# Product P1 of the gate is copied into the gate's PSUM bank, and nine matmuls accumulate on the copy

## The chip, the cores and the metric

The kernel runs on one core of a Trainium2 chip. The metric is the time of one execution on the device in microseconds (us), the median of three runs. Inside the core there are five engines with a program each, all in order: TensorE (PE, matrix products; its weight loads are listed apart as PEld), VectorE (DVE), ScalarE (ACT), GpSimd (POOL) and SyncE (SP). The last two mostly start transfers (DMA) here.

## The reference

The input x has 2048 tokens of 640 values. It is normalised (mean and variance per token), and three things are added: x itself, the real part of a two-dimensional Fourier transform of the normalised x, and a gated feed-forward layer of it.

```python
xn = layernorm(x)                                    # 2048 x 640
a, b = xn @ hid_re.T, xn @ hid_im.T                  # Fourier transform along the hidden axis
A = seq_re @ a - seq_im @ b                          # and along the tokens, real part
gate, up = xn @ W_gate, xn @ W_up                    # 640 x 1728 each
B = (relu(gate) * up) @ W_down                       # 1728 x 640
out = x + A + B
```

All is float32. The kernel keeps that precision by splitting each operand into a high and a low part and making three matmuls of one: high by high, high by low, low by high (`mm3`, lines 136 to 141).

## The kernel before

The program has three stages that follow each other on PE: the token transform (to 405 us of the profile), gate and up (405 to 730 us), and the last stage that multiplies by W_down and the hidden Fourier matrix and writes the output. The change is in the second.

**Gate and up** works through 26 units: 13 tiles of 128 columns of W_gate and W_up, for each half of the tokens. A unit computes a 128 x 1024 tile of relu(gate) * up. It does not make the block products one by one, but by a scheme of the Strassen-Winograd kind: sums and differences of the weight blocks (`Weights.sums`, five DVE operations on tile `z`, L861 to L865) and of the token blocks (made earlier, the tiles `xs_early`, `r` and `sets_b`) are multiplied, and the products are added in several ways. P1 = A11·B11 is such a product; it is needed in more than one result.

**One unit on PE** (`gate_up`, lines 917 to 968). A unit uses three PSUM banks, `b1`, `b2` and `b4`, 128 x 512 each. Its matmuls, in order: 6 into `b1` (P1); 9 into the `b1` of the unit before (`last_products(n - 1)`, not in unit 0); 9 into `b2` (A12·B21 and A4·X4); 9 into `b4` (S1·T1 and U4·X4); 6 on top of `b1` (S2·T2); 3 on top of `b4` (G4·X4); 6 on top of `b4` (S4·B22); 6 on top of `b1` (S3·T3). That is 54. Some of them cannot start before another engine has read the bank: the 6 of S2·T2 must wait for the copy of `b1`, and the 3 of G4·X4 for the copy of `b4` into `ob` (L954, shown as `ob<-ps` on ACT).

**One unit on ACT.** In this order: `copy(p1, b1)` (`p<-ps`, PSUM to SBUF), the high part of the next unit's weights in two pieces (`ahead.high(0)`, `gw<-z` of 1024 columns, and `ahead.high(1)`, `gw<-z` of 1152), `copy(ob, b4)`, `copy(u2, b1)` (`u<-ps`) and `copy(u3, b1)` (`u<-ps`). Between u3 and the next unit's p1 stand the ACT steps of side work: `besides[n]` and `urgent[n]`, which prepare tokens and weights for later (lines 1113 to 1132).

**One unit on DVE.** `ahead.sums()`; then `finals(n - 1)`, three operations that finish the unit before (L886 and twice L888: relu of the gate times up, for both column halves); then L945, which adds `b2` and p1 into the first half of `oa`; the low parts of the next unit's weights (`gw<-z,gw`, L875, twice; the second needs `ahead.high(1)`); L963, which adds `b4` and u2 into the second half of `oa`; then the side work of `besides[n]`.

**What sets the order.** PE, DVE and ACT are pinned to the order in which the program is written (`tc.manual_schedule(engines=PINNED)`, L1162). The Tile layer only adds the waits. The tiles p1, u2, u3 and oa come from pool `tmp` that has one buffer for each name (L839), so `oa` of unit n lies where `oa` of unit n - 1 lies, which `finals(n - 1)` still reads.

Of the kernel before, what the change touches and what calls it, by code (L numbers as in the profile page):

```python
# [10 lines left out]
OP = mybir.AluOpType  # L11
# [5 lines left out]
W2 = 2 * CH  # L17
# [19 lines left out]
B11, B12, B21, B22, T1, T2, T3, T4, X4 = range(9)  # L37
# [5 lines left out]
A11, A12, A22 = (2 * P * i for i in range(3))  # L43
A4, U4, G4 = (6 * P + P * i for i in range(3))
# [21 lines left out]
def fnet_reglu_kernel(  # L66
# [56 lines left out]
    def bank():  # L123
        return psum_p.tile([P, CH], F32, name="ps")
# [4 lines left out]
    def copy(o, i):  # L129
        return nc.scalar.activation(o, i, AF.Copy)  # L130
# [715 lines left out]
    tt = nc.vector.tensor_tensor  # L846
# [33 lines left out]
    tmp = lambda name, n=CH: pool("tmp").tile([P, n], F32, name=name)  # L880
    c0, c1 = slice(0, CH), slice(CH, W2)

    def finals(n):

        u3, oa, ob, b1 = held.pop(n)
        tt(ob[:, c1], ob[:, c1], u3, op=OP.add)  # L886
        for c, up in ((c1, ob[:, c1]), (c0, b1)):
            nc.vector.scalar_tensor_tensor(ob[:, c], oa[:, c], 0.0, up, op0=OP.max, op1=OP.mult)  # L888
        with tc.issue_after(nc.gpsimd.dma_start(hd[1 - n // NF][n % NF], ob).ins):
            for f in behind_store[n]:  # L890
                f()
# [3 lines left out]
    def products(n):  # L895

        q, w = 1 - n // NF, weights[n].w

        def block(ps, a, b, first, last, more=False):
            for j in range(2):  # L900
                o = a + j * P
                mm3(ps, (w[:, 0, o : o + P], w[:, 1, o : o + P]), set_half(q, b, j),
                    first and j == 0, last and j == 1, more)

        def block4(ps, a, c, last, more=False):
            mm3(ps, (w[:, 0, a : a + P], w[:, 1, a : a + P]), set_half(q, X4, c), False, last, more)

        return block, block4

    def last_products(n):  # L910

        block, block4 = products(n)
        b1 = held[n][-1]
        block(b1, A22, T4, False, False, True)
        block4(b1, U4, 0, True, True)

    def gate_up(n):
        ahead = weights.get(n + 1)

        def the_rest():  # L920
            if ahead:
                ahead.high(1)
                ahead.low(0)
                ahead.low(1)

        block, block4 = products(n)
        for f in issues[n]:
            f()
        b1, b2, b4 = bank(), bank(), bank()
        block(b1, A11, B11, True, True)  # L930
        if ahead:
            ahead.sums()
        if n > 0:
            last_products(n - 1)
            finals(n - 1)
        p1, u2, u3, oa = tmp("p1"), tmp("u2"), tmp("u3"), tmp("oa", W2)
        ob = pool("hob").tile([P, W2], F32, name="ob")
        for f in urgent[n]:
            f()
        copy(p1, b1)  # L940
        if ahead:
            ahead.high(0)
        block(b2, A12, B21, True, False)
        block4(b2, A4, 0, True)
        tt(oa[:, c0], b2, p1, op=OP.add)  # L945
        if n > 0:
            the_rest()
        if n + 2 < NU:
            weights[n + 2] = Weights(n + 2)
        for f in loads[n]:  # L950
            f()
        block(b4, S1, T1, True, False)
        block4(b4, U4, 1, True)
        copy(ob[:, c1], b4)  # L954
        if n == 0:
            the_rest()
        block(b1, S2, T2, False, True, True)
        copy(u2, b1)
        for f in midway[n]:
            f()  # L960
        block4(b4, G4, 1, False, True)
        block(b4, S4, B22, False, True, True)
        held["dve"] = tt(oa[:, c1], b4, u2, op=OP.add)  # L963
        block(b1, S3, T3, False, True, True)
        held["act"] = copy(u3, b1)
        for f in besides[n]:
            f()
        held[n] = u3, oa, ob, b1
# [193 lines left out]
    with tc.manual_schedule(engines=PINNED):  # L1162
        third[0]()
        fourth_set[0]()
        weights[0] = Weights(0)
        rest_weights()
        weights[1] = Weights(1)
        weights[0].high(0)
        weights[0].low(0)
        weights[0].sums()  # L1170
        third[1]()
        weights[0].high(1)
        weights[0].low(1)
        gate_up_rest(1, None)
        for n in range(NU):
            gate_up(n)
        for f in issues[NU]:
            f()
        gate_up_rest(0, NU - 1)
# [394 lines left out]
```

## Time and profile before

| what | value |
|---|---|
| time, median of 3 runs (lowest, highest) | 1022.85 us (1022.72, 1023.73) |
| span of the profiled execution, first to last instruction | 1021.1 us |
| outside the span, against the median | 1.75 us |
| PE busy | 1015.6 us, 4510 matmuls |
| DVE busy | 823.5 us |
| ACT busy | 454.9 us |
| gate and up | 405.2 to 730 us |

A row of the timeline is: start (us), duration (us), engine, line, operation, names of what is written and read, shapes, count, and in brackets the idle time of the engine just before, with the instruction that ended it. A row of the waits is: who waited for whom, total us, number of times, longest us. A row of a window is: the stretch, its length, busy time and instruction count of each engine, granted clock, DMA share, GB/s. Where matmuls follow each other without a gap, their starts are 0.227 us apart, though each is recorded with a duration of 0.39 us, since they overlap in the pipeline.

### The profile page before, as it was taken

The page shows a single profiled execution, that of the slowest core. Times are in us where ns is not written, and L with a number is a line of the kernel's source. Part 1 is how long each engine was busy: PE and PEld are TensorE (multiplying, and loading weights), DVE is VectorE, ACT ScalarE, POOL GpSimd, SP SyncE. Part 2 cuts the span into 40 slices and gives each one's busy share as a digit, 9 for nine tenths or more (in the row PEclk, how much of TensorE's full clock was granted, in tenths as well). Part 3 has the DMA queues.
Part 4 walks back from the last instruction along what each step waited for, and adds up shares of the span by engine and source line. Part 5 has one row for each costly group of instructions (what it writes and reads, how often), then busy time and mean ns, then how long its engine had stood idle before and what let it go on. Part 6 is the DMA issues. An engine that isn't in the chain of part 4 may idle for free.

```text
span 1021.1 us, 12761 instructions
## 1 busy us (share of the span) xinstructions
PE 1015.6 (99%) x4510; PEld 840.8 (82%) x4510; DVE 823.5 (81%) x1162; ACT 454.9 (45%) x588; POOL 117.2 (11%) x189
## 2 busy tenths in 40 slices
PE   9999999999999999999999999999999999999998
PEld 7888888888888888888888888888888888888887
DVE  7967976969979697688888977787597888589887
ACT  6664453333334444434445444443443454454552
POOL 2000010121110001321111111111100000000001
PEclk9999999999999999999999999999999999999999
DMA  9884744976869666874658989899798879999784
GB/s 336 314 270 173 265 149 142 330 259 200 348 210 340 222 190 224 261 232 167 232 208 286 285 295 316 289 341 313 234 335 250 256 249 325 328 326 315 219 284 165
DMA packets 113872, 267.57 MB, mean 262 GB/s; under 512 B 13104, under 2 KB 58096, under 8 KB 112176
## 3 DMA queue, kind: packets, MB, share of 16 engines
q1 hardware_dynamic: 92416, 179.03, 52.5%
q0 software_dynamic: 20960, 87.31, 24.6%
q8 instruction: 35, 0.57, 0.2%
q10 hardware_dynamic: 432, 0.43, 0.1%
q14 instruction: 29, 0.24, 0.1%
HBM read 203.26 MB, written 72.89 MB: 270 GB/s over the span
## 4 chain that ended last, share of the span: by engine, by line
PE 99%; DMA 0%; ACT 0%; DVE 0%; SPq 0%; issue 0%
PE ps L140 32%; PE ps L139 32%; PE ps L141 32%; PE ps L527 3%; PE ps L556 1%; PE ps L1368 1%; DMA raw<-in_dft 0%; ACT cb L357 0%; ACT xs_early L258 0%; DVE y L1225 0%; SPq L596 0%; ACT mv L234 0%
## 5 line engine op out<-in xcount | busy, mean ns | idle before, releaser
L139 PE MATMUL ps<-cb,wt 128*128 128x512 f32 (+1 forms) x407 | 157.9, 388 | 0.0
L141 PE MATMUL ps<-cb,wt 128*128 128x512 f32 (+1 forms) x407 | 157.9, 388 | 0.0
L140 PE MATMUL ps<-cb,wt 128*128 128x512 f32 (+1 forms) x407 | 157.9, 388 | 0.0
L133 ACT ACTIVATE cb<-rw 128x1024 fp32r<-128x1024 f32 (+1 forms) x94 | 89.2, 960 | 77.1 <-PE ps L141 56.5
L134 DVE TENSOR_TENSOR cb<-rw,cb 128x1024 fp32r<-128x1024 f32 (+1 forms) x94 | 102.6, 1101 | 22.3 <-ACT cb L133 21.7
L133 ACT ACTIVATE cb<-raw 128x1024 fp32r<-128x1024 f32 x64 | 67.9, 1061 | 105.2 <-PE ps L141 97.0
L134 DVE TENSOR_TENSOR cb<-raw,cb 128x1024 fp32r<-128x1024 f32 x64 | 78.2, 1222 | 31.5 <-ACT cb L133 31.3
L141 PE MATMUL ps<-xs_early,gw 128*128 128x512 f32 x260 | 101.2, 389 | 0.0
L139 PE MATMUL ps<-xs_early,gw 128*128 128x512 f32 x260 | 101.2, 389 | 0.0
L140 PE MATMUL ps<-xs_early,gw 128*128 128x512 f32 x260 | 101.1, 389 | 0.0
L139 PE MATMUL ps<-cb,xs_late 128*128 128x512 f32 x232 | 90.2, 389 | 0.0
L140 PE MATMUL ps<-cb,xs_late 128*128 128x512 f32 x232 | 90.2, 389 | 0.0
L141 PE MATMUL ps<-cb,xs_late 128*128 128x512 f32 x232 | 90.2, 389 | 0.0
L139 PEld LDWEIGHTS ps<-cb,wt 128*128 128x128 f32 x407 | 76.4, 188 | 16.0 <-DVE y L1225 0.2
L141 PEld LDWEIGHTS ps<-cb,wt 128*128 128x128 f32 x407 | 76.4, 188 | 15.7
L140 PEld LDWEIGHTS ps<-cb,wt 128*128 128x128 f32 x407 | 76.4, 188 | 15.6
L139 PE MATMUL ps<-cb,xs_early 128*128 128x512 f32 x226 | 87.9, 389 | 0.0
L140 PE MATMUL ps<-cb,xs_early 128*128 128x512 f32 x226 | 87.9, 389 | 0.0
L141 PE MATMUL ps<-cb,xs_early 128*128 128x512 f32 x226 | 87.9, 389 | 0.0
L130 ACT ACTIVATE gw<-z 128x1024 fp32r<-128x1024 f32 (+1 forms) x52 | 56.4, 1110 | 38.6 <-PE ps L141 23.6
L130 ACT ACTIVATE u<-ps 128x512 f32<-128x512 f32 x52 | 31.1, 598 | 89.6 <-PE ps L141 77.7
L875 DVE TENSOR_TENSOR gw<-z,gw 128x1024 fp32r<-128x1024 f32 (+1 forms) x52 | 64.8, 1284 | 1.9 <-ACT gw L130 1.8
(209 smaller groups left out, 1989.4 us busy)
## 6 DMA issues: line engine op xcount, KB each, us to landing
raw<-in_dft SPq DMA_DIRECT2D x94, 512.0 KB, 5.4
wt<-wparts SPq DMA_DIRECT2D x74, 256.0 KB, 4.3
wparts<-pw POOLq DMA_DIRECT2D x12, 1408.0 KB, 7.9
z<-in_wgu SPq DMA_DIRECT2D x26, 640.0 KB, 5.6
rw<-hd SPq DMA_DIRECT2D x27, 512.0 KB, 6.2
hd<-ob POOLq DMA_DIRECT2D x26, 512.0 KB, 4.8
wt<-wparts SPq DMA_DIRECT2D x29, 384.0 KB, 5.4
rw<-pq SPq DMA_DIRECT2D x19, 512.0 KB, 6.4
```

The lines of the kernel that those rows point to most:

```text
L130: return nc.scalar.activation(o, i, AF.Copy)
L133: nc.scalar.activation(hi, src, AF.Copy)
L134: return nc.vector.tensor_tensor(lo, src, hi.bitcast(F32), op=OP.subtract)
L139: nc.tensor.matmul(ps, wh, mh, start=first, stop=False, skip_group_check=more)
L140: nc.tensor.matmul(ps, wh, ml, start=False, stop=False, skip_group_check=more)
L141: nc.tensor.matmul(ps, wl, mh, start=False, stop=last, skip_group_check=more)
L527: nc.tensor.matmul(E[0, key], xn_part(n * SG + j, d)[v == 1], b[:, int(v == 2), j], start=False, stop=n % NH == NH - 1 and (j, v) == (SG - ...
L556: nc.tensor.matmul(E[c, key], xn_part(j, d)[v == 1], b[c][0][:, int(v == 2), j], start=j == 0 and v == 0, stop=False)
L875: tt(self.w[:, 1, cs], self.z[:, cs], self.w[:, 0, cs].bitcast(F32), op=OP.subtract)
L1368: nc.tensor.matmul(B[out], w[:, v, oo : oo + P], b, start=False, stop=last and v == 1, skip_group_check=more)
```

## The change

Tile p1 is left out. ACT's copy of `b1` goes into bank `b2` (PSUM to PSUM), and the nine matmuls into `b2` no longer clear the bank at their first one, but accumulate on the copy. The sum is then in `b2`, so that DVE's L945 is left out, and ACT copies `b2` into the first half of `oa`.

```diff
-        p1, u2, u3, oa = tmp("p1"), tmp("u2"), tmp("u3"), tmp("oa", W2)
+        u2, u3, oa = tmp("u2"), tmp("u3"), tmp("oa", W2)
         ob = pool("hob").tile([P, W2], F32, name="ob")
         for f in urgent[n]:
             f()
-        copy(p1, b1)
+        copy(b2, b1)
         if ahead:
             ahead.high(0)
-        block(b2, A12, B21, True, False)
-        block4(b2, A4, 0, True)
-        tt(oa[:, c0], b2, p1, op=OP.add)
+        block(b2, A12, B21, False, False, True)
+        block4(b2, A4, 0, True, True)
+        copy(oa[:, c0], b2)
         if n > 0:
             the_rest()
```

`the_rest` is `ahead.high(1)`, `ahead.low(0)` and `ahead.low(1)`. In unit 0 it stands behind `copy(ob, b4)` instead.

How the order moves is seen in unit 1. On ACT, before (p, gw and ob as above, u_3292 is u2, u_3293 is u3):

```order
L130 ACTIVATE p_3291<-ps 128x512 [waits DVE_49,PE_49]
L130 ACTIVATE gw<-z 128x1024 [waits DMAHW1_49,PE_49]
L130 ACTIVATE gw<-z 128x1152 [waits DVE_49]
L130 ACTIVATE ob<-ps 128x512 [waits DMASW5_49,DMASW3_49,DMASW6_49,DMASW2_49,DMASW7_49,DMASW0_49,PE_49]
L130 ACTIVATE u_3292<-ps 128x512 [waits PE_49,Activation_49]
L130 ACTIVATE u_3293<-ps 128x512 [waits DVE_49,PE_49]
```

And with the change:

```order
L130 ACTIVATE ps<-ps 128x512 [waits PE_49]
L130 ACTIVATE gw<-z 128x1024 [waits DMAHW1_49,PE_49,Activation_49]
L130 ACTIVATE oa<-ps 128x512 [waits DVE_49,PE_49,Activation_49]
L130 ACTIVATE gw<-z 128x1152
L130 ACTIVATE ob<-ps 128x512 [waits PE_49]
L130 ACTIVATE u_3290<-ps 128x512 [waits PE_49,Activation_49]
L130 ACTIVATE u_3291<-ps 128x512 [waits PE_49,Activation_49]
```

A copy into `oa` has come between the two pieces of the high weights, ahead of the copy into `ob`, and it waits for DVE (the second L888 of the unit before is what reads the old `oa` last) and for PE.

On DVE, from the finals of unit 0 to L963 of unit 1, before:

```order
L886 TENSOR_TENSOR ob<-ob,u_3200 128x512 [waits Activation_49]
L888 SCALAR_TENSOR_TENSOR ob<-oa,ob 128x512 [waits DVE_49]
L888 SCALAR_TENSOR_TENSOR ob<-oa,ps 128x512 [waits PE_49]
L945 TENSOR_TENSOR oa<-ps,p_3291 128x512 [waits DVE_49,PE_49,Activation_49]
L875 TENSOR_TENSOR gw<-z,gw 128x1024 [waits Activation_49]
L875 TENSOR_TENSOR gw<-z,gw 128x1152 [waits Activation_49]
L963 TENSOR_TENSOR oa<-ps,u_3292 128x512 [waits PE_49,Activation_49]
```

And with the change:

```order
L886 TENSOR_TENSOR ob<-ob,u_3199 128x512 [waits Activation_49]
L888 SCALAR_TENSOR_TENSOR ob<-oa,ob 128x512 [waits DVE_49]
L888 SCALAR_TENSOR_TENSOR ob<-oa,ps 128x512 [waits PE_49]
L875 TENSOR_TENSOR gw<-z,gw 128x1024 [waits Activation_49]
L875 TENSOR_TENSOR gw<-z,gw 128x1152 [waits Activation_49]
L963 TENSOR_TENSOR oa<-ps,u_3290 128x512 [waits DVE_49,PE_49,Activation_49]
```

Only L945 is gone. PE keeps its order, and its first matmul into `b2` in unit 1 gets a wait on ACT. The last matmul of `last_products` and the first two of `b2`, with the change:

```order
L141 MATMUL ps<-xs_early,gw 128x512
L139 MATMUL ps<-xs_early,gw 128x512 [waits Activation_49]
L140 MATMUL ps<-xs_early,gw 128x512
L141 MATMUL ps<-xs_early,gw 128x512
L139 MATMUL ps<-xs_early,gw 128x512
```

Before, the same rows stand there without a wait.

## The prediction

> **What bounds the kernel now.** I read the page's totals and its chain first, then PE's own waits, then two windows of one unit each in gate and up (unit 10, which runs latest against PE, and unit 15, a quiet one).
>
> ```profile
> PE 1015.6 (99%) x4510; PEld 840.8 (82%) x4510; DVE 823.5 (81%) x1162; ACT 454.9 (45%) x588; POOL 117.2 (11%) x189
> PE 99%; DMA 0%; ACT 0%; DVE 0%; SPq 0%; issue 0%
> PE ps L121 <- DVE warm L117: 1.1, 1, 1.1
> PE ps L556 <- ACT xs_early L258: 0.7, 1, 0.7
> 525.56:537.85 12.29, 12.29 (x56) 10.06 (x54) 10.64 (x21) 5.86 (x8) 1.84 (x3) 1.00 0.67 237
> 586.81:599.05 12.24, 12.24 (x56) 10.14 (x54) 9.70 (x18) 5.27 (x7) 1.98 (x3) 1.00 0.87 284
> ```
>
> PE carries 99% of the chain, and in the whole execution it waits twice, 1.8 us in all, both times before 7 us. So in gate and up it never waits. Two things follow. Taking work from DVE cannot make PE faster, since PE waits for nobody there and its matmuls stay the same in number and order. And every moment in which the change makes PE wait is added to the end in full, because nothing later has slack in which to lose it. The question is only where PE now waits, and how long.
>
> **The clock of a unit.** A unit's 54 matmuls take 12.24 us, 0.2267 each. Unit 1 and unit 25 start at these rows:
>
> ```profile
> 415.40 0.39 PE L139 MATMUL ps<-xs_early,gw 128*128 128x512 f32 x1
> 709.21 0.39 PE L139 MATMUL ps<-xs_early,gw 128*128 128x512 f32 x1
> ```
>
> Their distance is 24 units of 12.24, plus the 0.05 by which unit 10 is longer. So unit n starts at T(n) = 415.40 + 12.24(n - 1), and 0.05 later from unit 11 on. By the counts in the program, `b2`'s nine matmuls start at T+3.40, the last of them at T+5.21, and G4's, which wait for the copy of `b4` into `ob`, at T+8.84. All times below are from T. Unit 10 (T = 525.56) shows how near ACT is to that edge already:
>
> ```profile
> 530.07 0.58 ACT L130 ACTIVATE p<-ps 128x512 f32<-128x512 f32 x1
> 530.54 1.05 ACT L130 ACTIVATE gw<-z 128x1024 fp32r<-128x1024 f32 x1
> 532.28 0.28 DVE L865 TENSOR_TENSOR z<-z 128x128 f32<-128x128 f32 x1
> 532.59 1.17 ACT L130 ACTIVATE gw<-z 128x1152 fp32r<-128x1152 f32 x1 [1.00 <-DVE z L865]
> 533.67 0.58 ACT L130 ACTIVATE ob<-ps 128x512 f32<-128x512 f32 x1
> 534.30 0.19 PEld L139 LDWEIGHTS ps<-xs_early,gw 128*128 128x128 f32 x1 [0.16 <-ACT ob L130]
> 534.40 0.39 PE L139 MATMUL ps<-xs_early,gw 128*128 128x512 f32 x1
> ```
>
> The copy into `ob` ends at 534.25; the weight load of G4 starts 0.05 later, its matmul 0.15 after the copy's end, at T+8.84, just on time. I take 0.16 from the end of an ACT copy to the matmul it releases. The rows also give ACT's pitch when it is back to back: an instruction starts 0.09 to 0.11 before the one ahead is recorded as ended (530.54 against 530.65; 533.67 against 533.76), and its delay behind a DVE end: 0.03 (L865 ends at 532.56, the second `gw<-z` starts at 532.59).
>
> **What is removed.** L945, 26 times:
>
> ```profile
> L945 DVE TENSOR_TENSOR oa<-ps,p 128x512 f32<-128x512 f32 x26 | 18.0, 692 | 7.3 <-PE ps L141 4.6
> L130 ACT ACTIVATE ob<-ps 128x512 f32<-128x512 f32 x26 | 15.5, 597 | 42.7 <-PE ps L141 42.7
> ```
>
> That is 18.0 us of DVE, and worth nothing by itself: PE hides it. Added are 26 ACT copies, PSUM to SBUF as the `ob` ones, so 0.6 each. ACT's total (45% of the span) has room. What counts is where the copy stands and what it waits for.
>
> **New wait 1: the copy into b2.** PE's first matmul of `b2` now needs the copy of `b1`. From unit 1 on, the nine matmuls of the unit before stand between (2.04 us). In unit 0 they do not:
>
> ```profile
> 406.76 0.60 ACT L130 ACTIVATE p<-ps 128x512 f32<-128x512 f32 x1 [0.76 <-PE ps L141]
> 406.56 0.39 PE L139 MATMUL ps<-xs_early,gw 128*128 128x512 f32 x1
> ```
>
> The copy ends at 407.36, PE can go on at 407.52 in place of 406.56: 0.96 us. A copy from PSUM to PSUM stands nowhere in the trace; it could take less than 0.6, hardly more than L945's 0.69, which moves this term by 0.1 at most. In later units the copy must end by T+3.24. In the latest, unit 10, it ends at 530.65, T+5.09: 1.85 late, because ACT does side work ahead of it.
>
> **New wait 2: the copy into oa.** It waits for the second L888 of the unit before, and behind it in ACT's queue are the second piece of high weights and then the copy into `ob`, for which PE's G4 waits. Before, nothing in front of `ob` on ACT waited for L888. If L888 ends at T+fe: the oa copy starts at fe + 0.03 (the delay behind a DVE end), the weights 0.50 later (0.59 less the 0.09 of overlap), the `ob` copy 1.08 after that (1.17 less 0.09), it takes 0.58, and PE goes on 0.16 later: fe + 2.35. PE should go on at 8.84. So PE stalls by fe - 6.49. The second L888 of each unit that comes near it (units 3 and 5 to 15):
>
> ```profile
> 446.38 0.68 DVE L888 SCALAR_TENSOR_TENSOR ob<-oa,ps 128x512 f32<-128x512 f32 x1
> 471.85 0.68 DVE L888 SCALAR_TENSOR_TENSOR ob<-oa,ps 128x512 f32<-128x512 f32 x1
> 483.06 0.68 DVE L888 SCALAR_TENSOR_TENSOR ob<-oa,ps 128x512 f32<-128x512 f32 x1
> 496.34 0.68 DVE L888 SCALAR_TENSOR_TENSOR ob<-oa,ps 128x512 f32<-128x512 f32 x1
> 509.14 0.68 DVE L888 SCALAR_TENSOR_TENSOR ob<-oa,ps 128x512 f32<-128x512 f32 x1
> 519.22 0.68 DVE L888 SCALAR_TENSOR_TENSOR ob<-oa,ps 128x512 f32<-128x512 f32 x1
> 533.81 0.68 DVE L888 SCALAR_TENSOR_TENSOR ob<-oa,ps 128x512 f32<-128x512 f32 x1
> 543.55 0.68 DVE L888 SCALAR_TENSOR_TENSOR ob<-oa,ps 128x512 f32<-128x512 f32 x1
> 557.19 0.68 DVE L888 SCALAR_TENSOR_TENSOR ob<-oa,ps 128x512 f32<-128x512 f32 x1
> 569.43 0.68 DVE L888 SCALAR_TENSOR_TENSOR ob<-oa,ps 128x512 f32<-128x512 f32 x1
> 580.76 0.68 DVE L888 SCALAR_TENSOR_TENSOR ob<-oa,ps 128x512 f32<-128x512 f32 x1
> 592.33 0.68 DVE L888 SCALAR_TENSOR_TENSOR ob<-oa,ps 128x512 f32<-128x512 f32 x1
> ```
>
> With their T, fe is 7.18, 8.17, 7.14, 8.18, 8.74, 6.58, 8.93, 6.38, 7.78, 7.78, 6.87 and 6.20. Some of this lateness is inherited: DVE comes late out of the unit before. A stall of PE there takes that part away, since DVE's L963 at the end of a unit then waits for PE again. L963 of units 5, 7, 8, 9 and 13:
>
> ```profile
> 475.68 0.68 DVE L963 TENSOR_TENSOR oa<-ps,u 128x512 f32<-128x512 f32 x1
> 500.16 0.68 DVE L963 TENSOR_TENSOR oa<-ps,u 128x512 f32<-128x512 f32 x1
> 512.96 0.68 DVE L963 TENSOR_TENSOR oa<-ps,u 128x512 f32<-128x512 f32 x1
> 524.47 0.69 DVE L963 TENSOR_TENSOR oa<-ps,u 128x512 f32<-128x512 f32 x1 [1.34 <-PE ps L141]
> 574.17 0.69 DVE L963 TENSOR_TENSOR oa<-ps,u 128x512 f32<-128x512 f32 x1
> ```
>
> Unit 9 is on time (T+11.15, DVE waits for PE); the others are at 11.32, 11.32, 11.88 and 11.84, late by 0.17, 0.17, 0.73 and 0.69. I take that off fe of units 6, 8, 9 and 14: 6.97, 8.57, 5.85, 6.18. The stalls by fe - 6.49 are then: unit 3 0.69, unit 5 1.68, unit 6 0.48, unit 7 1.69, unit 8 2.08, unit 10 2.44, units 12 and 13 1.29 each, the rest none; 11.64 in all. Units 16 to 24 do the same work as unit 15, with 0.29 to spare. Wait 1 is not added in these units: a stall at `b2` shifts G4's due time by as much, while the finals do not wait for `b2`, so the larger of the two counts (in unit 10, 2.44 over 1.85).
>
> After a hold-up PE needs a few matmuls to regain its pace; unit 10, where only a weight load was held, is 0.05 longer than unit 15 in the windows above. For nine stalls that is 0.45.
>
> **Sum.** 0.96 + 11.64 + 0.45 = 13.05 us. The profiled execution's span was 1021.1, so the new span is 1034.15; the median of the runs lies 1.75 above the span: 1035.9 us, 1.3% slower.
>
> What is late next: the second low part of the weights, on DVE behind the second high piece.
>
> ```profile
> L875 DVE TENSOR_TENSOR gw<-z,gw 128x1024 fp32r<-128x1024 f32 (+1 forms) x52 | 64.8, 1284 | 1.9 <-ACT gw L130 1.8
> ```
>
> It can start when that piece ends, at fe + 0.03 + 0.50 + 1.17 = fe + 1.70, and ends about 1.3 later, in unit 10 at 11.9; the next unit needs it at 12.24 plus the stall of 2.44: hidden, with over 2 us. The stores of `ob` follow the finals as before. No DMA is added or moved.
>
> **Rivals.**
>
> *Lateness cures itself.* If fe is late only because DVE trails from unit to unit, the first stalls let it catch up and later units find it on time: 0.96 + 0.69 = 1.7, so 1024.5 us, no difference. Units 6, 8, 9 and 14 speak for it. Against it: L963 of unit 9 waited 1.34 us for PE, so DVE was on time, and yet unit 10 has the latest fe; its lateness is made inside the unit, by side work. It decides if the same held for units 5, 7 and 12. 5%.
>
> *The freed 0.69 moves the finals.* If L945's time came off fe in each unit, the stalls would be 0, 0.99, 0, 1.00, 1.39, 1.75, 0.60, 0.60, 6.3 in all; with unit 0 and seven restarts 7.6, so 1030.5. Against it: between L945 and the next finals stands L963, which mostly waits for PE. 11%.
>
> *The chain from L888 to G4 is longer than by rows.* Each 0.1 on it costs eight stalls 0.1, and beyond 0.29 units 14 to 24 pay too: with 0.6 more, 8 x 0.6 + 11 x 0.3 = 8.1, so 1044; with 0.3 more, 1038.3. Nothing in the rows asks for it, but an ACT copy that waits for DVE and PE at once is not among them. 10%.
>
> *The clock drops.* The first matmuls of the execution run at half the pace of those that follow, and the column of the granted clock does not tell it:
>
> ```profile
> 1.05:4.45 3.40, 3.40 (x33) 3.40 (x34) 0.74 (x2) 1.49 (x2) 0.00 (x0) 1.00 0.75 213
> 4.45:5.29 0.84, 0.84 (x17) 0.82 (x15) 0.77 (x4) 0.63 (x3) 0.00 (x0) 1.00 0.98 246
> 6.20:10.20 4.00, 4.00 (x18) 3.27 (x19) 3.68 (x11) 2.38 (x6) 1.43 (x2) 1.00 1.04 407
> ```
>
> 33 matmuls of 128 columns in 3.40 us, then 17 in 0.84. If each of nine stalls led to 3.4 us at half pace, each would cost 1.7 more, 15 in all: 1051. Against it: after the 0.7 us wait at L556 the third window has 18 of 512 columns in 4.00 us, the full pace. [...] 3%.
>
> *Faster* would need PE to have waited before, and it did not: 1%.
>
> **How the numbers follow.** Forecast 1035.9 with 70%; its own uncertainty is 0.1 to 0.2 of a us on each of eight stalls and the inherited parts (had they not gone, 0.17 + 0.17 + 0.09 + 0.38 more), so 1034 to 1038. The range takes in the freed 0.69 below and the longer chain above: 1030 to 1041. A measurement of this kernel tells about 0.2% (2 us) from no change. Slower by more: 94%; within: 5%; faster: 1%.
>
> **What would show it.** In the new profile PE's waits list ACT: in unit 0 the `ps<-ps` copy, 0.7 to 1.0; in units 5, 7, 8, 10, 13 the same copy, and then in those and in 3, 6, 12 the `ob` copy. The `oa` copy's idle time is ended by DVE L888 in units 3 to 13 and by L888 too in 15 to 24, with no stall behind it. PE outside gate and up keeps its times. I would be wrong if quiet units stall, if matmuls after a stall start more than 0.24 apart, or if L888 moves against T.

## The result and the profile after

The changed kernel takes 1036.47 us (median of four runs, 1036.19 to 1036.78) against 1022.98 us before (four runs, 1022.72 to 1023.73): a ratio of 1.0129, 95% interval 1.0115 to 1.0144. The forecast was 1035.9 us in a range of 1030 to 1041. The profiled execution's span is 1034.4 us, 13.3 more than before.

The changed kernel's page (busy times, chain of waits), PE's waits (who waited for whom, total us, times, longest), and two groups of instructions (busy, mean ns, idle time just before and what ended it), with the row of L963 before the change behind them:

```profile
PE 1020.7 (99%) x4510; PEld 841.0 (81%) x4510; DVE 808.4 (78%) x1136; ACT 466.7 (45%) x614; POOL 117.3 (11%) x189
PE 90%; DVE 5%; ACT 2%; issue 2%; DMA 0%; POOL 0%; ACTq 0%; DVEq 0%; POOLq 0%
PE ps L139 <- ACT ps L130: 5.6, 6, 1.6
PE ps L139 <- ACT ob L130: 3.3, 7, 1.0
L130 ACT ACTIVATE oa<-ps 128x512 f32<-128x512 f32 x26 | 15.6, 599 | 51.4 <-DVE ob L888 43.6 <-PE ps L141 7.9
L963 DVE TENSOR_TENSOR oa<-ps,u 128x512 f32<-128x512 f32 x26 | 18.0, 691 | 48.2 <-PE ps L141 47.0 <-issue 1.2
```

```profile
L963 DVE TENSOR_TENSOR oa<-ps,u 128x512 f32<-128x512 f32 x26 | 17.9, 690 | 34.6 <-PE ps L141 34.6
```

DVE has become 15 us lighter and spends what it gained in waiting: its idle time before L963 went from 34.6 to 48.2 us. PE, which waited for nobody in gate and up, now waits for the two ACT copies that were named, 13 times. The chain of waits, 99% PE before, now passes through DVE and ACT for 7% of the span, with 2% of issue beside them. The two rows of waits sum to 8.9 us and not 13.3. Most of the difference is that they begin at the recorded end of the last matmul, 0.16 us after the next one was due, and that the matmul behind a wait is followed by the next only 0.34 us later in place of 0.23: for 13 waits that is 3.5 us of the 4.4.

Unit 10 in the timeline of the changed kernel (start, duration, engine, line, names; T = 533.51):

```profile
538.08 0.58 ACT L130 ACTIVATE ps<-ps 128x512 f32<-128x512 f32 x1
538.71 0.50 PE L139 MATMUL ps<-xs_early,gw 128*128 128x512 f32 x1 [1.64 <-ACT ps L130]
539.05 0.40 PE L140 MATMUL ps<-xs_early,gw 128*128 128x512 f32 x1
541.81 0.68 DVE L888 SCALAR_TENSOR_TENSOR ob<-oa,ps 128x512 f32<-128x512 f32 x1
542.60 0.60 ACT L130 ACTIVATE oa<-ps 128x512 f32<-128x512 f32 x1 [2.97 <-DVE ob L888]
543.10 1.16 ACT L130 ACTIVATE gw<-z 128x1152 fp32r<-128x1152 f32 x1
544.15 0.59 ACT L130 ACTIVATE ob<-ps 128x512 f32<-128x512 f32 x1
544.79 0.50 PE L139 MATMUL ps<-xs_early,gw 128*128 128x512 f32 x1 [0.31 <-ACT ob L130]
```

The path is the one that was worked out: the second L888 ends at 542.49, the `oa` copy starts 0.11 behind it, then the second piece of the high weights, then the `ob` copy, which ends at 544.74, and G4's matmul comes 0.05 later. ACT stood idle for 2.97 us until DVE was done, and then `ob` still had two instructions ahead of it. A window of unit 10 and one of unit 15, and ACT in unit 15 (T = 600.08):

```profile
533.51:548.33 14.82, 12.88 (x56) 9.98 (x55) 10.96 (x22) 6.26 (x9) 1.84 (x3) 1.00 0.62 216
600.08:612.32 12.24, 12.24 (x56) 10.13 (x54) 9.10 (x17) 5.68 (x8) 1.98 (x3) 1.00 0.94 284
606.37 0.60 ACT L130 ACTIVATE oa<-ps 128x512 f32<-128x512 f32 x1 [1.63 <-DVE ob L888]
607.92 0.59 ACT L130 ACTIVATE ob<-ps 128x512 f32<-128x512 f32 x1
```

Unit 15 still takes 12.24 us. Its `ob` copy ends at T+8.43 and could end at T+8.68.

The time that each unit lost (its length against 12.24 us, unit 0 against 10.20):

| unit | 0 | 3 | 5 | 6 | 7 | 8 | 10 | 12 | 13 | others | sum |
|---|---|---|---|---|---|---|---|---|---|---|---|
| forecast, with 0.05 for each restart | 1.01 | 0.74 | 1.73 | 0.53 | 1.74 | 2.13 | 2.49 | 1.34 | 1.34 | 0 | 13.05 |
| measured | 0.97 | 0.75 | 1.75 | 0.56 | 1.75 | 2.15 | 2.57 | 1.41 | 1.39 | 0 | 13.30 |

### The profile page after: what moved, and what is told of

The parts are those of the page before. It is cut to its first block, busy times and chain, and to the rows that moved or that the text cites. A ratio compares the mean times of both kernels' runs of the same rounds, so it can differ in the third digit from the quotient of the medians.

```text
span 1034.4 us, 12733 instructions
## 1 busy us (share of the span) xinstructions
PE 1020.7 (99%) x4510; PEld 841.0 (81%) x4510; DVE 808.4 (78%) x1136; ACT 466.7 (45%) x614; POOL 117.3 (11%) x189
## 4 chain that ended last, share of the span: by engine, by line
PE 90%; DVE 5%; ACT 2%; issue 2%; DMA 0%; POOL 0%; ACTq 0%; DVEq 0%; POOLq 0%
PE ps L139 28%; PE ps L141 28%; PE ps L140 28%; PE ps L527 3%; DVE ob L888 1%; ACT gw L130 1%; PE ps L556 1%; PE ps L1368 1%; PE ps L121 1%; DVE ob L886 0%; ACT ob L130 0%; DVE sets_b L440 0%; DVE z L862 0%; DVE pw L134 0%; DMA hd<-ob 0%
## 5 line engine op out<-in xcount | busy, mean ns | idle before, releaser
L875 DVE TENSOR_TENSOR gw<-z,gw 128x1024 fp32r<-128x1024 f32 (+1 forms) x52 | 66.9, 1288 | 22.3 <-ACT gw L130 22.2
```

The source lines that it names most:

```text
L875: tt(self.w[:, 1, cs], self.z[:, cs], self.w[:, 0, cs].bitcast(F32), op=OP.subtract)
```

## Experiments

The theory has three claims: what costs time is PE's wait for two ACT copies and nothing in the accumulation itself; the `ob` copy is late because the `oa` copy, which waits for DVE's finals, stands ahead of it in ACT's queue; and in a unit the larger of the two waits counts, not their sum. The rivals: accumulating on a bank that ACT wrote is slow in itself; ACT's added work, not the wait, delays `ob`; DVE's freed time is worth something; the clock falls behind PE's pauses.

**The oa copy moved back.** Against the changed kernel:

```diff
-        copy(oa[:, c0], b2)
         if n > 0:
             the_rest()
...
         copy(u2, b1)
+        copy(oa[:, c0], b2)
```

> As the changed kernel, but the copy of b2 into oa stands on ACT behind the copies into ob and u2. Theory (the ob copy is late because it queues behind an oa copy that waits for the finals on DVE): PE's waits for `ob` all go; the waits for the copy into b2 stay, by their measured sizes with restart 0.94 in unit 0, 1.1 in units 5 and 7, 1.2 in unit 8, 1.9 in unit 10, 0.95 in unit 13, together 7.2 to 7.4: 1030.3 us. Rival (accumulating on a bank that ACT has written costs PE by itself, wherever the copy stands): no change from 1036.5.

Measured: 1031.19 us, 1.0076 times the kernel before (1.0061 to 1.0091). PE's waits in it:

```profile
PE ps L139 <- ACT ps L130: 5.5, 6, 1.6
```

The waits for `ob` are gone, those for the `b2` copy are what they were. The units lose 0.97 (unit 0), 1.11, 1.13, 1.26, 1.95 and 0.99 (units 5, 7, 8, 10, 13), 7.5 us with 0.04 in unit 12 and 0.02 in unit 6. The nine matmuls still accumulate on ACT's copy in all 26 units; that costs nothing.

**Two buffers for the first half of oa.** The order of the changed kernel is kept, the wait is taken away by giving the copy another place to write to (`finals` and L963 then use the pair's members):

```diff
-        u2, u3, oa = tmp("u2"), tmp("u3"), tmp("oa", W2)
+        u2, u3, oa = tmp("u2"), tmp("u3"), (tmp(f"oc{n % 2}"), tmp("oa"))
...
-        copy(oa[:, c0], b2)
+        copy(oa[0], b2)
```

> As the changed kernel with the same order on ACT, but the first half of oa has two buffers used in turn, so that the copy into it need not wait for the finals of the unit before. Theory: the wait and not the place is what delays ob, so the time is that of the kernel with the oa copy moved back, 1030.3 us, with PE waiting for the b2 copy alone (7.2 to 7.4). If 0.6 us more work in ACT's queue ahead of ob were the cause by itself, the waits for ob would stay and the time near 1036.5.

Measured: 1030.92 us, 1.0072 (1.0057 to 1.0087), 7.45 us lost in the units, again with one row of waits of PE in gate and up:

```profile
PE ps L139 <- ACT ps L130: 5.5, 6, 1.6
```

So the copy's place and its 0.6 us of work are harmless; the wait for the finals, in that place, is what cost.

**DVE makes the copy into oa.** The seed in PSUM alone, without the ACT copy:

```diff
-        copy(oa[:, c0], b2)
+        nc.vector.tensor_copy(oa[:, c0], b2)
```

> As the changed kernel, but DVE copies b2 into oa, in the place where it added before; ACT has the copy into b2 alone. Theory: half of the change, the seed in PSUM, with the waits for the b2 copy only, 7.2 to 7.4: 1030.3 us; that DVE has its 0.69 us per unit back costs nothing. Rival (freed DVE time is worth something): slower than the kernel with the oa copy moved back.

Measured: 1030.84 us, 1.0073 (1.0056 to 1.0090), 7.46 us lost in the units. PE's row of waits for the `b2` copy is the same as in the two above (5.5 us, 6 times), and the time cannot be told from theirs, though DVE makes a copy more in each unit.

**The ACT copy into oa alone.** Against the kernel before, so that `b2` starts anew and p1 stays:

```diff
-        tt(oa[:, c0], b2, p1, op=OP.add)
+        copy(oa[:, c0], b2)
+        tt(oa[:, c0], oa[:, c0], p1, op=OP.add)
```

> The other half alone: p1 stays in SBUF, the nine matmuls start the bank anew, ACT copies b2 into oa in the place that the change gives it, and DVE adds p1 to oa in L945's place. Theory: PE waits for ob alone, by fe - 6.49 plus restart: 11.6 + 0.6 = 12.2, so 1035.2 us, nearly all of the change's cost; with the other half's 7.3 the two halves sum to 19.5, against 13.5 for both, because in a unit the larger wait counts and not their sum. If they added up, the whole change would have cost 19.5.

Measured: 1036.87 us, 1.0131 (1.0116 to 1.0146), 1.7 more than expected. In the profiled execution the units lose 0.77 (unit 3), 1.75, 0.57, 1.75, 2.15 (5 to 8), 1.37 and 1.37 (12, 13) as expected, and unit 10 4.09 in place of 2.5. Its PE rows around the wait, and two windows of 6 us, one from that wait on and one of quiet work before it:

```profile
542.07 0.39 PE L141 MATMUL ps<-r,gw 128*128 128x512 f32 x1
544.71 0.80 PE L139 MATMUL ps<-xs_early,gw 128*128 128x512 f32 x1 [2.26 <-ACT ob L130]
545.30 0.63 PE L140 MATMUL ps<-xs_early,gw 128*128 128x512 f32 x1
545.73 0.63 PE L141 MATMUL ps<-xs_early,gw 128*128 128x512 f32 x1
548.39 0.39 PE L139 MATMUL ps<-r,gw 128*128 128x512 f32 x1
548.62 0.40 PE L140 MATMUL ps<-r,gw 128*128 128x512 f32 x1
544.71:550.71 6.00, 6.00 (x20) 4.79 (x21) 3.12 (x7) 1.11 (x3) 0.00 (x0) 0.73 0.86 295
520.00:526.00 6.00, 6.00 (x29) 4.95 (x28) 5.74 (x12) 2.26 (x3) 0.77 (x1) 1.00 0.60 206
```

Behind the wait the matmuls start 0.43 us apart, for 3.3 us, and then 0.23 again; the granted clock of that window is 0.73. This is the rival of the falling clock, in a kernel where it had not been looked for. Of the four timed executions two have a mean granted clock of 0.998 and took 1037.48 and 1038.16 us, two have 1.000 and took 1035.58 and 1036.27. Without the fall the units lose 13.83 - 1.55 = 12.3, as expected. The halves thus cost 7.5 and 12.3 us, 19.8 together, and the whole change 13.3: the larger wait of a unit counts, not the sum. It holds unit by unit: unit 5 loses 1.11 and 1.75 in the halves and 1.75 in the whole, unit 8 1.26 and 2.15, and 2.15 in the whole.

**b2 behind b4.** PE's order is changed, and ACT copies into `oa` behind `ob`:

```diff
-        block(b2, A12, B21, False, False, True)
-        block4(b2, A4, 0, True, True)
-        copy(oa[:, c0], b2)
         if n > 0:
             the_rest()
...
         block(b4, S1, T1, True, False)
         block4(b4, U4, 1, True)
+        block(b2, A12, B21, False, False, True)
+        block4(b2, A4, 0, True, True)
         copy(ob[:, c1], b4)
+        copy(oa[:, c0], b2)
```

> As the changed kernel, but PE does b4's nine matmuls ahead of b2's nine, and the copy into oa stands on ACT behind the one into ob. The copy into b2 then has 2.04 us more, 9 matmuls in unit 0 and 18 in the others, to T+5.28; the latest one before ended at T+5.09. Theory: no waits of PE in gate and up, 1023.0 us, the same as before the change, with 18 us less on DVE. Rival (accumulation on a copy is slower in itself): slower than before by up to 13 us.

Measured: 1023.33 us against 1023.32, a ratio of 0.9999 (0.9990 to 1.0009). Its busy times and all of PE's waits:

```profile
PE 1015.7 (99%) x4510; PEld 840.6 (82%) x4510; DVE 806.5 (79%) x1136; ACT 467.4 (46%) x614; POOL 117.2 (11%) x189
PE ps L121 <- DVE warm L117: 1.1, 1, 1.1
PE ps L556 <- ACT xs_early L258: 0.8, 1, 0.8
```

Same work as in the changed kernel, the same seed in PSUM, 17 us less on DVE than before, and no wait in gate and up (unit 10 alone is 0.08 longer than 12.24, as its `ob` copy ends at T+8.75). It gives back the whole loss and gains nothing: DVE's time was never what PE waited for.

**One more ACT copy behind the one into oa.**

```diff
         copy(oa[:, c0], b2)
+        copy(p1, b2)
```

> As the changed kernel, with one more ACT copy of b2 (into scratch) right behind the one into oa: 0.50 us more in the chain from the second L888 to G4. Theory: the eight late units stall 0.5 longer, 4.0; in quiet units the ob copy of the changed kernel ends at T+8.43 and may end at T+8.68, so the 11 units 14 to 24 stall by 0.25 plus a restart, 0.3 each, 3 in all: 1043.5 us. Rival (ACT has room, 45% busy): no change from 1036.5.

Measured: 1044.01 us, 1.0201 (1.0185 to 1.0216). Its rows of PE's waits for the two copies:

```profile
PE ps L139 <- ACT ob L130: 7.3, 8, 1.5
PE ps L139 <- ACT ps L130: 5.6, 6, 1.6
```

Units 3, 5 to 8, 10, 12 and 13 lose 0.46 to 0.53 us more each, and units 14 to 24, which lost nothing, 0.27 to 0.29 each. So in the changed kernel the quiet units stood 0.25 us from the edge, and the edge is where the rows put it. That ACT is busy for only 45% of the span protected nothing.

**Long waits.** In two quiet units PE is made to wait longer:

```diff
+        for _ in range({18: 20, 22: 10}.get(n, 0)):
+            copy(p1, b1)
         copy(b2, b1)
```

> As the changed kernel, but in unit 18 twenty and in unit 22 ten ACT copies into scratch stand ahead of the copy into b2, so that PE waits for some 9 to 13 us and 4 to 6 us there. It asks what a long wait does to the pace behind it. If the clock is not affected: matmuls 0.227 apart behind both waits but for the first two. If it falls after long idleness, as at the start of the execution: about 3.4 us of matmuls 0.43 apart, 1.7 us more behind each. The nine waits of 0.5 to 2 us in the changed kernel show no such pace.

The two waits, and the matmuls behind them:

```profile
651.52 0.80 PE L139 MATMUL ps<-xs_early,gw 128*128 128x512 f32 x1 [11.11 <-ACT ps L130]
652.12 0.63 PE L140 MATMUL ps<-xs_early,gw 128*128 128x512 f32 x1
652.54 0.63 PE L141 MATMUL ps<-xs_early,gw 128*128 128x512 f32 x1
707.42 0.80 PE L139 MATMUL ps<-xs_early,gw 128*128 128x512 f32 x1 [4.80 <-ACT ps L130]
708.01 0.63 PE L140 MATMUL ps<-xs_early,gw 128*128 128x512 f32 x1
708.44 0.63 PE L141 MATMUL ps<-xs_early,gw 128*128 128x512 f32 x1
```

Both are followed by matmuls 0.43 apart, 9 of them behind the wait of 11.1 us and 14 behind that of 4.8. The execution took 1058.75 us.

**Graded waits, twice.** The same loop, with 5 copies in units 15, 17 and 24, 6 in 16, 18, 20 and 22, 7 in 19 and 21 and 8 in 23; the same kernel ran twice.

> As the changed kernel, with 5 to 8 ACT copies into scratch ahead of the copy into b2 in units 15 to 24, so that PE waits there, at 0.63 us a copy, for some 1.85 (units 15, 17, 24), 2.5 (16, 18, 20, 22), 3.1 (19, 21) and 3.75 us (23); 25 us more in all, 1061.9 with no loss of pace. It asks from which length a wait is followed by matmuls at half pace (1.6 us more each time), which the half with oa copied by ACT alone showed behind a wait of 2.4 us in unit 10 in its profiled execution. [...] If it depends on where a fixed raster of time lies against the wait: some of the 2.5 and 3.1 us waits and not others, and none at 1.85.

> The same kernel a second time. If a length decides, the same units lose their pace; if the place of a raster decides, partly others.

They took 1072.95 and 1073.55 us. How many waits were followed by some 3.4 us or more at half pace (lengths by the time between the matmuls' starts, less 0.23):

| wait | 1.8 to 1.9 us | 2.5 us | 3.1 us | 3.8 us |
|---|---|---|---|---|
| first execution | 0 of 3 | 3 of 4 | 2 of 2 | 1 of 1 |
| second execution | 0 of 3 | 2 of 4 | 2 of 2 | 1 of 1 |

Unit 22 has the same wait in both; the first execution loses its pace there, and the second does not. The wait's row and the window of 6 us behind it, from the first and then from the second:

```profile
716.84 0.50 PE L139 MATMUL ps<-xs_early,gw 128*128 128x512 f32 x1 [2.35 <-ACT ps L130]
716.84:722.84 6.00, 6.00 (x19) 4.79 (x20) 2.71 (x3) 2.57 (x3) 1.23 (x2) 0.72 0.84 295
```

```profile
717.26 0.50 PE L139 MATMUL ps<-xs_early,gw 128*128 128x512 f32 x1 [2.35 <-ACT ps L130]
717.26:723.26 6.00, 6.00 (x26) 4.99 (x27) 2.85 (x3) 3.39 (x5) 1.22 (x2) 1.00 0.86 289
```

So the length alone does not decide at 2.5 us, and here the slow pace began six matmuls behind the wait. The starts of the matmuls show what tells the cases apart. Apart from the 0.34 us right behind each wait, a step clearly between 0.23 and 0.43 us means that the pace changed inside it. Unit 18 of the first execution has one at each end of its slow stretch, 0.38 and 0.27 us:

```profile
649.91 0.58 PE L140 MATMUL ps<-xs_early,gw 128*128 128x512 f32 x1
650.29 0.63 PE L141 MATMUL ps<-xs_early,gw 128*128 128x512 f32 x1
653.28 0.44 PE L139 MATMUL ps<-sets_b,gw 128*128 128x512 f32 x1
653.55 0.40 PE L140 MATMUL ps<-sets_b,gw 128*128 128x512 f32 x1
```

By the share of such a step at each pace, an estimate from these rows, the pace falls at 649.96 and returns at 653.37. Worked out in the same way, it falls in units 18 to 23 at 649.96, 667.04, 684.08, 701.16, 718.22 and 735.29 us. These are 17.04 to 17.08 apart, five times 3.41, though the ends of the waits are 16.5 to 17.8 apart; and it returns 3.41 to 3.43 us after each fall. The second execution has a raster of 3.41 us too, at another place: none of the 21 changes of pace in both lies more than 0.03 us off its raster. In these two executions the cases are told apart by the part of a wait that lies inside one interval of the raster: in all eleven in which the pace fell, that was 2.03 us or more, and in the nine others it was 1.82 or less. Unit 22 waited 2.03 of its 2.51 us in one interval in the first execution, and 1.57 and 0.94 in two intervals in the second. This bound was read from the two executions afterwards and not tried on a third; what sets the raster, the runs do not show.

## Why the prediction was right

- *PE waits for nobody, so nothing can be gained and each wait counts in full.* Right. The kernel with `b2` behind `b4` has all of DVE's relief and PE unhindered, and it takes the time of before; each wait that came back is found in the end.
- *New wait 1, unit 0: 0.96.* Measured 0.97. The copy from PSUM to PSUM takes 0.58 us in the mean, where the one from PSUM to SBUF took 0.59; the bounds set for it held.
- *New wait 2: PE goes on at fe + 2.35.* Right as a path, and the runs separate its parts: the wait for the finals (two buffers), the place ahead of `ob` (copy moved back) and the slope (one more copy, 0.46 to 0.53 for a pitch of 0.50). The spare time of the quiet units was put at 0.29 and was 0.25. One term was too small: the `oa` copy starts 0.11 to 0.12 us behind the end of L888 in all units that wait for it, where 0.03 was taken from a copy of weights that waits for DVE alone; the step from the weights to `ob` was 1.05, not 1.08.
- *The chain from L888 to G4 is longer than by rows*, 10%: so in kind, an ACT copy that waits for DVE and PE being the one that the rows lacked, but by about 0.05 us net and not 0.3 or 0.6. Why it starts later was not separated.
- *Inherited lateness goes.* fe fell to 6.96 in unit 6, 8.55 in unit 8, 5.83 in unit 9 and 6.18 in unit 14, where 6.97, 8.57, 5.85 and 6.18 were forecast. The cause given, a stall of PE, is enough: the same happens where DVE has no time freed (DVE makes the copy). But it is not needed: with `b2` behind `b4` PE never waits in these units, and fe still is 6.98, 8.56, 5.84 and 6.29. There the freed 0.69 lets DVE catch up. The changed kernel has both. The rival that all lateness cures itself fell with unit 10, whose fe rose from 8.93 to 8.98 although DVE came out of unit 9 on time.
- *The larger wait counts.* Right, by the two halves: 7.5 and 12.3 apart, 13.3 together.
- *Release 0.16 and restart 0.05 a stall.* Right in sum. The first matmul comes 0.05 us behind the copy's end, and the ones behind it are 0.13 to 0.16 late in all, 0.11 of it in the first step (0.34 us): 0.18 to 0.22, where 0.21 was summed. Units 12 and 13 lost 1.41 and 1.39 where 1.34 was summed; most of that is the longer start of the `oa` copy. Since one step of 0.34 is part of each release, the sign that was to speak against the forecast (matmuls over 0.24 apart behind a stall) was badly put.
- *The freed 0.69 moves the finals* fell: in units 3, 5, 7, 10, 12 and 13, where fe is not inherited, it moved by 0.05 us at most (8.17 to 8.15 in unit 5, 7.78 to 7.78 in unit 12). It moves only what was inherited, as above.
- *The clock drops*, 3%: it did not in the profiled execution of the changed kernel (mean granted clock 1.000), but the argument against it was too weak. It rested on a wait of 0.7 us, and the waits that were forecast reach 2.4, while later runs show the drop behind 5 of 8 waits of 2.5. What protected the changed kernel was that unit 10's loss of 2.57 us falls into two waits, 1.8 us at `b2` and 0.5 at G4, with a restart each; neither lowered the pace (granted clock 1.00 in the window of unit 10), nor did any of the six graded waits of 1.8 to 1.9. The kernel with the second half alone takes it in one piece of 2.4 us and paid 1.55 more in the profiled execution. Of its four timed executions two have a mean granted clock of 0.998 (1037.48 and 1038.16 us) and two 1.000 (1035.58 and 1036.27 us), so not every one pays. The forecast's statement that the column of the granted clock does not tell of it holds for the start of the execution; in gate and up the column showed 0.72 and 0.73.

## What to carry to other kernels

Where one engine carries the whole chain and never waits, as PE did in gate and up, look for no gain from moving work between the others: 17 us off DVE gave none (1023.33 us against 1023.32), and two new waits cost 13.3. Ask of each new dependence of that engine when it will be met in the latest stretch, not in the mean one. A single-buffered destination makes a harmless copy wait for its old readers, and in an engine that works in order everything behind that copy waits too, even when its busy share is 45%: 13.30 us were lost in the units here, 7.45 with two buffers. If such a seed in PSUM is wanted, put enough matmuls between the copy and the first one that adds to it: nine more were enough here, with no wait of PE in gate and up.

## What the hardware showed that was not expected

PE fell to half pace behind waits of 2.5 us in 5 of 8 cases, behind all six of 3.1 us and more with graded copies and both of 4.8 and 11.1 us, and behind none of the six of 1.8 to 1.9 us. In the 20 graded waits it fell when 2.03 us or more of the wait lay inside one interval of a raster of 3.41 us, and not when 1.82 or less did; it fell at the end of that interval, in unit 22 of the first execution 1.4 us behind the wait. The slow stretch was 0.43 us a matmul for one interval of about 3.4 us (8 matmuls, 1.6 us lost) behind most. Behind the wait of 4.8 us and one of 3.8 it was 14 matmuls: counted back from the return of the pace, an estimate by the raster, these waits reached 0.65 to 0.68 us into the next interval, and the slow pace lasted to the end of the one after that. The shortest wait with a slow stretch behind it was the one of 2.4 us in the kernel with the second half alone: 2.26 us lie there between the recorded end of one matmul and the start of the next.
